# Second LayerNorm of rows 512 to 1023: from the tail into the segment loop

## The chip, the core and the metric

The kernel runs on one core of one Trainium2 chip. The metric is the device time of one execution in microseconds (us); smaller is better. The engines named below are PE (TensorE, matmuls; PEld is its weight load), DVE (VectorE), ACT (ScalarE), POOL (GpSimd) and SP (SyncE, which here only issues DMAs).

## The reference

What is computed is one transformer layer on x, 2048 rows of 640, in bf16. The first half is attention with a recurrent memory: the rows are taken in 64 segments of 32, each segment's 8 memory rows are the first 8 output rows of the segment before, so the segments must run one after the other. The second half is a LayerNorm and a gated feed-forward network over all rows.

```python
for s in range(n_seg):                      # 64 segments of 32 rows, in order
    h = concat([mem, layernorm(x)[segment s]])
    q, k, v = h @ Wq, h @ Wk, h @ Wv        # 32 heads of 128
    o = softmax(mask(q @ k.T * scale)) @ v @ Wo
    mem = o[:, :8]                          # goes into segment s + 1
    outs.append(o[:, 8:])
h  = x + concat(outs)                       # 2048 x 640
n  = layernorm(h)                           # the second LayerNorm
h2 = h + (relu(n @ W_gate) * (n @ W_up)) @ W_down     # 640 -> 1728 -> 640
```

## The kernel before

Every operation is recorded with the tiles that it reads and writes (`add`, `dma`), and `_Graph.solve` turns these into semaphore waits. Each engine then runs its own operations strictly in the order in which they were recorded. So the order of the Python statements is the order of each queue, SP's among them: a DMA that has to wait holds up every DMA recorded behind it on SP.

**The segment loop** (L1119 to L1297) runs s from 1 to 63, straight-line code, one segment a step. A step projects the keys (L1157), finishes the previous segment's attention over its own rows (`pv_x`, L1172, which reads V through the tile VM), projects the queries and values, takes scores, and multiplies with Wo (`wo_split`, `wo_pass`). The chain from one step to the next goes through `fold_split` (L635): DVE transposes into TA (L637), ACT copies into SA (L639), POOL or DVE adds (L641), and `to_act_split` (L650) writes the 8 memory rows of the next step's input. VM is filled by DMAs from SP (`merge_v`, L683, called at L1235): three DMAs, due at `pv_x` of the next step. PE is kept filled within a step by other work (`filler`, and matmuls that `fill_of` splits in two).

**Early row groups.** Rows 0 to 511, as four groups of 128 rows, get their second LayerNorm inside this loop. A group begins at a step e of `EARLY` (L981) and takes five steps:

- step e, near its end (L1271): SP loads the group's x rows into xt and its attention output into at;
- step e + 1 (L1174): POOL adds them into xt (`add_attn`, L730), SP stores the sum to the DRAM tensor h_d, and at the end of the step DVE takes the row statistics (`row_moments`, L1285);
- step e + 2 (L1169): ACT and POOL scale the rows (`row_std`, `row_scale`);
- step e + 4 (L1242, L1269): SP transposes xt into at by a transposing DMA, and then stores at to the DRAM tensor xn2_d. The store writes runs of 128 elements.

The tile at is shared: the first LayerNorm's rows go through it in steps with s % 4 == 1, and the attention load of a group overwrites it.

POOL's other work in a step is `late_q` (L518, for the next step's scores), `late_o` (L598) and, where s % 4 is not 1, the addition L641 of the chain. In the order of POOL these stand behind `add_attn`, and on SP `merge_v` of the same step stands behind the store to h_d.

**The last steps.** From step 49 on xn2_d is read back (`early_rows`, L908) for early pieces of the first gate and up products, and before the end of the loop all of it goes into the tile xn2T0 (L1190).

**The tail.** The feed-forward part runs over four blocks of 512 rows. For block b, `gate_up(b, j)` makes 14 column tiles from the tile xn2T (L1014, L1027), and `down_pair` multiplies with Wd (L1311, L1324), adds the residual rows in h_rows (`down_out`, L1333) and stores. Block 1 takes its input from xn2T1 and its residual from h1. Its four row groups, 4 to 7, are prepared while block 0 runs: `ln2_load` brings x and the attention output (tiles xt2, at2), `ln2_front` adds, takes statistics and scales (DVE L730, L356, L358, L370, ACT L361, L363), `ln2_back` transposes into xn2T1 by a transposing DMA (L375). The calls for groups 4 to 7 stand at L1403, L1415, L1416, L1431, L1440, L1441, L1450 and L1451, between the gate and up products of block 0, its weight loads (`load_down`, `load_piece`) and its down products. Blocks 2 and 3 are prepared in the same manner during blocks 1 and 2 (L1423, L1442); the change leaves these alone.

Of the kernel before, what the change touches and what calls it, by code (L numbers as in the profile page):

```python
# [5 lines left out]
BF16 = mybir.dt.bfloat16  # L6
# [171 lines left out]
def build_kernel(nc, A_x, A_mem0, A_Wq, A_Wk, A_Wv, A_Wo, A_seg_len, B_W_gate, B_W_up, B_W_down, out):  # L178
    _, S, D = A_x.shape
# [6 lines left out]
    DC = D // 128  # L186
# [8 lines left out]
    CH = [8 * g + 4 * hf + f for hf in range(2) for g in range(4) for f in range(4)]  # L195

    x_ap, out_ap, mem0_ap = A_x[0], out[0], A_mem0[0]
    h_d = nc.dram_tensor("h_d", [TB, D], BF16)
    xn2_d = nc.dram_tensor("xn2_d", [128, DC, TB], BF16)
    attn_d = nc.dram_tensor("attn_d", [S, 4, DC * 32], BF16)  # L200
    ends_d = nc.dram_tensor("ends_d", [128, 64 * H + 8 * VW], BF16)
    NE = 7
# [148 lines left out]
    def dma(dst, src, r=(), w=(), eng="sp"):  # L351
        add(eng, lambda e: e.dma_start(dst, src), r=r, w=w, dma=True)  # L352
# [384 lines left out]
    def ln2_load(i):  # L737
        u = i % 4
        dma(xt2[u][:, :], x_ap[128 * i:128 * i + 128, :], r=[("Wdone", 1)], w=[("xt2", u)])
        load_attn(at2[u], i, [("Wdone", 1)], ("at2", u))  # L740

    def ln2_front(i):
        par, u = (i // 4) % 2, i % 4
        h, hk = h_rows[par][:, u, :], ("h", par, u)
        add_attn(h, xt2[u], at2[u], [("xt2", u), ("at2", u)], [hk])
        row_stats(h, hk, 128)
        row_scale(h, hk, 128, xt2[u], ("xt2", u))
# [160 lines left out]
    def early_rows(q, lo, hi):  # L908
        ks = [XHOME[q][c][1] for c in range(lo, hi)] + ([("Ve1", q)] if hi == DC else [])
        if q:  # L910
            dst = ends[:, 512 * lo:512 * hi].rearrange("p (c t) -> p c t", t=512)
        elif hi == DC:
            dst = XHOME[0][4][0].rearrange("p (c t) -> p c t", t=512)
        else:
            dst = (Ke[0], Qe[0])[lo // 2][:].rearrange("p h t -> p (h t)").rearrange("p (c t) -> p c t", t=512)
        dma(dst, xn2_d[:, lo:hi, :], r=[("xn2_d", u) for u in range(4)], w=ks)

    def early_tile(s, q):
        return ((xt, ("xt",)), (at, ("at",)) if s < NSEG - 7 else (xl, ("xl",)))[q]
# [58 lines left out]
                    flip(2 + i, (Qe, Ke)[j][p], i, [(("Qe", "Ke")[j], p, i)])  # L978
        return part, evac

    EARLY = (15, 23, 31, 39)  # L981

    def woe_sum(bk):

# [134 lines left out]
    for s in range(1, NSEG):  # L1119
# [16 lines left out]
        if s > 0:  # L1136
            a, ks = pass_act(s)
            held, parts = fill_of(s)
            if s in (NSEG - 14, NSEG - 13, NSEG - 10, NSEG - 9, NSEG - 5, NSEG - 4):
                early_weights(s, 1)  # L1140
            elif s in (NSEG - 12, NSEG - 8):
                q = 1 - place(s)[0]
                for n in range(2):
                    dma((ends[:, 1024 * n:1024 * n + 1024] if q else (Ke, Qe)[n][0][:].rearrange("p h t -> p (h t)")),
                        next_d[2 * q + n][:, :], r=[("next", 2 * q + n)] + [("next", 3, i) for i in range(2) if q * n],
                        w=[(("Ke", "Qe")[n], q, i) for i in range(2)])
                add("pool", lambda p, q=q: p.memset(ap(Ve[q], Dh, [[VW, 8], [1, VW - Dh]]), 1.0),
                    w=[("Ve1", q), ("Ve", q, 0), ("Ve", q, 1)])
            elif s == NSEG - 3:
                for n in range(2):  # L1150
                    dma(ends[:, 1024 * n:1024 * n + 1024], ends_d[:, 1024 * n:1024 * n + 1024], r=[("ends",)],
                        w=END_KEYS[2 * n:2 * n + 2])
            elif s == 1:
                dma(ends_d[:, :], ends[:, :], r=END_KEYS, w=[("ends",)])
                far_save(0)
                far_save(1)
            for i in range(2):  # L1157
                project(a, ks, 1, (i,), ((P2, P3)[i],), *WAYS[i], held=i == 1 and held[0], parts=parts[i])
                to_tok((P2, P3)[i], i, "act")
                if last and i == 1:  # L1160
                    load_piece(("Ko", 0), "act")
                flip(i, Ko, i, [("Ko", i)])
            if s == 1:
                row_std(n_rows(1))
                row_scale(xl, ("xl",), n_rows(1), xl, ("xl",), "pool")
            if s % 4 == 2 and more:
                row_std(n_rows(nb + 1))
                row_scale(xl, ("xl",), n_rows(nb + 1), xl, ("xl",), "pool")
            if s % 4 == 1 and e2 is not None:  # L1169
                row_std(128)  # L1170
                row_scale(xt, ("xt",), 128, xt, ("xt",), "pool")
            pv_x(s - 1, 0)  # L1172
            norm_x(0)
            if s % 4 == 0 and e2 is not None:  # L1174
                add_attn(xt[:, :], xt, at, [("xt",), ("at",), ("rx",)], [("xt",)], "pool")
                dma(h_d[128 * e2:128 * e2 + 128, :], xt[:, :], r=[("xt",)], w=[("h_d", e2)])
            if s % 4 == 2:
                merge_v(s, 1)
            if not last:
                for i in range(2):  # L1180
                    project(a, ks, 0, (i,), ((P0, P1)[i],), *WAYS[i], held=i == 1 and held[1], parts=parts[2 + i])
                    to_tok((P0, P1)[i], 2 + i, "act")
                    flip(2 + i, Qo, i, [("Qo", i)])
                    if i == 0:
                        norm_x_late(0)
                        flip_ox(s - 1, (0,))
            else:
                norm_x_late(0)
                flip_ox(s - 1, (0,))
            if s == NSEG - 2:  # L1190
                for n, (lo, hi) in enumerate(((0, 1), (1, 2), (2, 3), (3, DC))):
                    dma(xn2T[0][:, lo:hi, :], xn2_d[:, lo:hi, :], r=[("xn2_d", u) for u in range(4)] + [("Wdone", 0)],
                        w=[("xn2", 0, n)])
            project(a, ks, 2, (0,), (P2,), range(4), held=not last and held[2])
            scores(s, 0, (0, 1))
            project(a, ks, 2, (0,), (P2,), (4,))
            scores(s, 0, (2, 3))
            if not last:
                exp_mem(s, 0)
                first_exp = G.ops[-1]  # L1200
                mask_mem(s, 0)
            to_v(P2, Vp, 0, ("Vp",), "act")
            if last:
                load_piece(("Vp", 0), "act")
            if s % 4 == 1 and ln:
                flip_rows(chunks_of(at[:, :]), xl, ("xl",), ("at",))
                if more:
                    ln1_load(nb + 1, xl, ("xl",))
                    G.ops[-1].after = first_exp
            if s in (NSEG - 15, NSEG - 11, NSEG - 7):  # L1210
                early_weights(s + 1, 0)
                G.ops[-1].after = first_exp
                early_rows(1 - place(s + 1)[0], 2, 4)
            elif s == NSEG - 3:
                dma(ends[:, 2048:], ends_d[:, 2048:], r=[("ends",)], w=END_KEYS[4:])
# [151 lines left out]
    def load_down(n):  # L1367
# [3 lines left out]
        if n == 4:  # L1371
            for q in range(2):
                dma(Wd[FR * q:FR * q + FR, FC - 1, :], B_W_down[FM:F, :], r=r, w=[("Wd", 5 + q)])

    s = NSEG - 1

    def rows(bk, p, s):
# [22 lines left out]
    flip_ox(s)  # L1400
    late_o(s)
    gate_up(0, NE + 2)
    ln2_load(4)  # L1403
    dma(hT[0][:, 0:NE, :], hx_d[:, :, :], r=[("Wdone", 2)] + [("hx", n) for n in range(NE)],
        w=[("hT", 0, n) for n in range(NE)])
    load_down(2)
# [5 lines left out]
            r=[("Wt", q, 0)], w=[("Wt", q, 1)])  # L1412
    load_down(3)
    load_down(4)
    ln2_load(5)  # L1415
    ln2_front(4)  # L1416
    rows(P2, (s + 1) % 2, s)
    woe_pass(P3, range(16))
    woe_sum(P3)
# [2 lines left out]
    for b in range(NBLK):  # L1422
        if 0 < b < NBLK - 1:  # L1423
            for u in range(4):
                ln2_load(4 * (b + 1) + u)
        for j in range(FC):
            p = j - NE if b == 0 else j
            if b or p > 3:
                gate_up(b, j)
            if b == 0 and p in (4, 5):  # L1430
                ln2_load(p + 2)  # L1431
            if b == 0 and p == 5:
                dma(h_rows[0][:, :, :], h_d[:, :].rearrange("(u p) d -> p u d", p=128), r=[("h_d", u) for u in range(4)] +
                    [("Wdone", 1), ("hT", 0, j)], w=[("h", 0, u) for u in range(4)])
            if b == 0 and p in (5, 6):
                load_piece(("hT", 0, j - 1))
                load_piece(("hT", 0, j - 1))
            if b == 0 and p in (4, 5):
                if p == 4:
                    ln2_front(5)  # L1440
                ln2_back(p, None)  # L1441
            if 0 < b < NBLK - 1:  # L1442
                fronts, backs = (1, 3, 5, 7), (3, 5, 7, 9)
                if p in fronts:
                    ln2_front(4 * (b + 1) + fronts.index(p))
                if p in backs:
                    ln2_back(4 * (b + 1) + backs.index(p), None)
        if b == 0:
            for u in (6, 7):
                ln2_front(u)  # L1450
                ln2_back(u, None)  # L1451
        assert not pieces
        for n in range(2):
            down_pair(b, n)
# [63 lines left out]
```

## Time and profile before

| what | value |
|---|---|
| three runs | 988.79, 989.08 and 992.45 us; median 989.08 us |
| profiled execution | span 990.5 us from first to last instruction; the page gives no other time for it |
| PE busy | 962.9 us, 97% |
| DVE, ACT, POOL busy | 714.3, 522.2 and 171.7 us |
| steps of the loop | about 12.1 us each |

The profile shows one execution. Its page gives the busy time of each engine, a strip of 40 slices of the span, the DMA queues, the chain of work that ended last, and groups of instructions by line; views of the trace behind it show the instructions in order of time, who waited for whom, and busy times in chosen stretches. The span lies 1.4 us above the median of the three runs and inside their range, so differences below are worked out inside this execution and then taken off the median.

### The profile page before, as it was taken

What the parts mean: (1) busy time and instruction counts of PE and PEld (TensorE: products, weight loads), DVE (VectorE), ACT (ScalarE), POOL (GpSimd) and SP (SyncE); (2) the same over time, 40 slices, a digit from 0 to 9 for tenths busy, and PEclk for the clock granted to TensorE, in tenths of its full rate; (3) what the DMA queues carried; (4) which work ended last, traced back from release to release, by engine and by line L of the source; (5) the groups of instructions that cost most, each with busy time, mean ns of one, the idle gap of its engine ahead of it and who ended that gap; (6) DMA issues with size and microseconds to landing.
All of it is one profiled execution on the core that took longest, in us unless ns stands there. A gap on an engine that the chain in (4) does not pass through costs nothing.

```text
span 990.5 us, 56552 instructions
## 1 busy us (share of the span) xinstructions
PE 962.9 (97%) x26159; PEld 530.9 (54%) x24953; DVE 714.3 (72%) x1860; ACT 522.2 (53%) x1326; POOL 171.7 (17%) x420
## 2 busy tenths in 40 slices
PE   4889999999999999999999999999999999999998
PEld 1335555555555656555555555555555565344443
DVE  3668787878887888788888878787877775545332
ACT  1456666666666666666666666656555552122120
POOL 7121112121302131213021302020201110000000
PEclk9999999999999999999999999999999999999999
DMA  9951112121222122212221221132323348613100
GB/s 358 416 200 39 43 40 48 34 54 49 54 42 54 50 59 45 54 49 54 42 54 49 54 47 49 35 106 61 103 62 99 84 129 255 203 21 94 27 14 27
DMA packets 84562, 83.10 MB, mean 84 GB/s; under 512 B 49562, under 2 KB 68834, under 8 KB 82402
## 3 DMA queue, kind: packets, MB, share of 16 engines
q1 hardware_dynamic: 82592, 78.53, 27.3%
q8 instruction: 201, 3.29, 1.3%
q10 hardware_dynamic: 1730, 0.96, 0.4%
q14 instruction: 39, 0.32, 0.1%
HBM read 44.02 MB, written 9.31 MB: 54 GB/s over the span
## 4 chain that ended last, share of the span: by engine, by line
PE 89%; SPq 5%; DMA 3%; DVE 2%; issue 1%; ACT 0%; POOL 0%; DVEq 0%; ACTq 0%; POOLq 0%
PE ps L414 46%; PE ps L1014 9%; PE ps L609 7%; PE ps L626 7%; PE ps L387 6%; SPq L352 5%; PE ps L669 3%; PE ps L1311 2%; PE ps L510 2%; PE ps L698 2%; DMA Wo<-in_A_Wo_dram 2%; PE ps L904 2%; PE ps L563 2%; DMA xn2T<-xt 1%; DMA VM<-Vp 0%
## 5 line engine op out<-in xcount | busy, mean ns | idle before, releaser
L414 PE MATMUL ps<-W,act_r 128*32 128x512 bf16 (+1 forms) x8383 | 462.2, 358 | 1.2 <-DVE act_r L650 0.8
L414 PEld LDWEIGHTS ps<-W,act_r 128*32 128x32 bf16 x8383 | 214.7, 96 | 171.3 <-DVE act_r L650 30.6
L438 ACT ACTIVATE tok<-ps 128x512 bf16<-128x512 f32 x182 | 105.2, 594 | 57.5 <-PE ps L414 50.6
L433 DVE STREAM_TRANSPOSE Ko<-tox 128x512 bf16<-128x512 bf16 x128 | 89.9, 703 | 44.3 <-ACT tox L438 44.0
L438 ACT ACTIVATE tox<-ps 128x512 bf16<-128x512 f32 x138 | 81.8, 598 | 62.3 <-PE ps L414 49.4
L414 PE MATMUL ps<-W,act_e 128*32 128x512 bf16 x1056 | 103.3, 383 | 4.1 <-DVE TBf L491 1.9
L589 DVE STREAM_TRANSPOSE oT<-tox 128x512 bf16<-128x512 bf16 x128 | 95.4, 745 | 0.0
L433 DVE STREAM_TRANSPOSE Qo<-tok 128x512 bf16<-128x512 bf16 x124 | 85.5, 689 | 1.2 <-ACT tok L438 0.5
L609 PE MATMUL ps<-Wo,oT 128*32 128x160 bf16 x4032 | 81.4, 233 | 3.1 <-DMA Wo<-in_A_Wo_dram 3.1
L626 PE MATMUL ps<-Wo,oT 128*32 128x320 bf16 x2016 | 79.8, 299 | 0.3 <-issue 0.3
L609 PEld LDWEIGHTS ps<-Wo,oT 128*32 128x32 bf16 x4032 | 70.4, 97 | 13.2 <-DMA Wo<-in_A_Wo_dram 3.7
L438 ACT ACTIVATE Vp<-ps 128x512 bf16<-128x512 f32 x127 | 75.2, 592 | 0.5 <-ACT Vp L438 0.5
L387 PE MATMUL ps<-W,act_e 128*32 128x512 bf16 x744 | 73.3, 384 | 0.0
L639 ACT ACTIVATE SA<-TA 64x40 f32<-64x40 f32 x126 | 29.5, 234 | 75.3 <-DVE TA L637 74.6
L1042 ACT ACTIVATE g<-ps 128x512 bf16<-128x512 f32 x45 | 26.1, 593 | 73.8 <-PE ps L1014 72.3
L526 ACT ACTIVATE Pm<-ps 128x64 bf16<-128x64 f32 x126 | 28.1, 223 | 67.0 <-PE ps L510 66.9
L583 DVE STREAM_TRANSPOSE oT<-om 128x128 bf16<-128x128 bf16 x126 | 39.2, 311 | 31.0 <-ACT om L575 31.0
L626 PEld LDWEIGHTS ps<-Wo,oT 128*32 128x32 bf16 x2016 | 53.2, 96 | 15.5 <-DVE rm L573 0.8
L510 PE MATMUL ps<-Qo,Ko 128*32 128x40 bf16 x2048 | 61.1, 181 | 0.0
L510 PEld LDWEIGHTS ps<-Qo,Ko 128*32 128x32 bf16 x2048 | 46.2, 94 | 25.8 <-DVE Qo L433 18.3
L1043 DVE TENSOR_TENSOR hT<-g,ps 128x512 bf16<-128x512 bf16 x45 | 30.9, 687 | 39.7 <-PE ps L1014 35.7
L518 POOL COPY Qo<-ends 128x256 bf16<-128x256 bf16 x32 | 14.0, 439 | 259.6 <-DVE oT L583 242.1
(159 smaller groups left out, 1494.6 us busy)
## 6 DMA issues: line engine op xcount, KB each, us to landing
VM<-Vp SPq DMA_DIRECT2D x126, 65.0 KB
VM<-Vp SPq DMA_DIRECT2D x63, 130.0 KB
W<-in_A_Wk_dram SPq DMA_DIRECT2D x5, 1024.0 KB
W<-in_A_Wq_dram SPq DMA_DIRECT2D x5, 1024.0 KB
W<-in_A_Wv_dram SPq DMA_DIRECT2D x5, 1024.0 KB
Wo<-in_A_Wo_dram SPq DMA_DIRECT2D x8, 640.0 KB
attn_d<-wtok SPq DMA_DIRECT2D x248, 7.5 KB
xt<-in_A_x_dram SPq DMA_DIRECT2D x16, 160.0 KB
```

The source lines that it names most:

```text
L352: add(eng, lambda e: e.dma_start(dst, src), r=r, w=w, dma=True)
L387: return pe.add_instruction(mybir.InstMatmult(name=nc.get_next_instruction_name(), engine=mybir.EngineType.PE, ins=[pe.lower_ap(rhs), pe.l ...
L414: ins = pe.matmul(*b, start=(c == ends[0]), stop=(c == ends[1]), skip_group_check=True)
L433: add("dve", lambda v: v.transpose(dst[:, 16 * i:16 * i + 16, 0:32], tok[t][:, :].rearrange("p (h f) -> p h f", f=32)), r=tok_keys(t), w=keys)
L438: add("act", lambda a: a.activation(dst, src, ACTF.Copy), r=r, w=w)
L510: i = pe.matmul(bank((P0, P1)[hf])[q:q + 32, o:o + 40], (Ko if a == 0 else Ke[p])[:, h, :], Qo[:, h, :], start=True, stop=True, skip_group ...
L583: add("dve", lambda v: v.transpose(ap(oT[par], 160 * hf, [[40, 4], [320, 4], [1, 8]]), ap(om, 128 * hf, [[1, 4], [4, 32]])), r=[("om", hf) ...
L589: add("dve", lambda v, kh=kh: v.transpose(ap(oT[p], 160 * kh + M, [[320, 4], [40, 4], [1, 32]]), ap(tox, 128 * kh, [[256, 4], [1, 4], [4, ...
L609: i = pe.matmul(bank(bk)[32 * gg:32 * gg + 32, 0:160], src[:, hb, 0:32], w[:, gg], start=(hb == CH[16 * halves[0]]), stop=(hb == CH[-1]), ...
L626: i = pe.matmul(bank(bk)[32 * q:32 * q + 32, 0:320], src[:, hb, 0:32], w, start=(n == 0), stop=(n == 7), skip_group_check=True)
L1014: ins = pe.matmul(bank(bk), w[:, c, lo:lo + 128], xn2T[par][:, c, :], start=(c == 0), stop=(c == DC - 1))
L1043: add("dve", lambda v: v.tensor_tensor(hT[par][:, j, :], g1[gi][:, :], bank(bu), ALU.mult), r=[B(bu), ("g1", gi)], w=[("hT", par, j)])
```

## The change

Four more groups, rows 512 to 1023, are prepared in the loop: `EARLY` gets a group every four steps from 15 to 43, where it had one every eight from 15 to 39. h_d and xn2_d grow to 1024 rows; reads of the first block's part of xn2_d take the slice 0:TB. In the tail, everything that prepared groups 4 to 7 goes (the loads, the additions, statistics and scaling, the transposes), and two DMAs take its place: one loads xn2T1 whole from xn2_d, one loads h1 from h_d. With the new spacing a group's last step is the first step of the next one: the transpose and the store of the one and the loads of the other then stand one behind the other on SP.

```diff
-    h_d = nc.dram_tensor("h_d", [TB, D], BF16)
-    xn2_d = nc.dram_tensor("xn2_d", [128, DC, TB], BF16)
+    h_d = nc.dram_tensor("h_d", [2 * TB, D], BF16)
+    xn2_d = nc.dram_tensor("xn2_d", [128, DC, 2 * TB], BF16)
...
-        dma(dst, xn2_d[:, lo:hi, :], r=[("xn2_d", u) for u in range(4)], w=ks)
+        dma(dst, xn2_d[:, lo:hi, 0:TB], r=[("xn2_d", u) for u in range(4)], w=ks)
...
-    EARLY = (15, 23, 31, 39)
+    EARLY = tuple(range(15, 47, 4))
...
-                    dma(xn2T[0][:, lo:hi, :], xn2_d[:, lo:hi, :], r=[("xn2_d", u) for u in range(4)] + [("Wdone", 0)],
+                    dma(xn2T[0][:, lo:hi, :], xn2_d[:, lo:hi, 0:TB], r=[("xn2_d", u) for u in range(4)] + [("Wdone", 0)],
...
+    def load_rows(b, r):
+        dma(h_rows[b][:, :, :], h_d[TB * b:TB * b + TB, :].rearrange("(u p) d -> p u d", p=128),
+            r=[("h_d", 4 * b + u) for u in range(4)] + r, w=[("h", b, u) for u in range(4)])
...
     gate_up(0, NE + 2)
-    ln2_load(4)
     dma(hT[0][:, 0:NE, :], hx_d[:, :, :], r=[("Wdone", 2)] + [("hx", n) for n in range(NE)],
...
     load_down(4)
-    ln2_load(5)
-    ln2_front(4)
+    dma(xn2T[1][:, :, :], xn2_d[:, :, TB:2 * TB], r=[("Wdone", 2)] + [("xn2_d", u) for u in range(4, 8)],
+        w=[("xn2", 1, u) for u in range(4)])
     rows(P2, (s + 1) % 2, s)
...
-            if b == 0 and p in (4, 5):
-                ln2_load(p + 2)
             if b == 0 and p == 5:
-                dma(h_rows[0][:, :, :], h_d[:, :].rearrange("(u p) d -> p u d", p=128), r=[("h_d", u) for u in range(4)] +
-                    [("Wdone", 1), ("hT", 0, j)], w=[("h", 0, u) for u in range(4)])
+                load_rows(0, [("Wdone", 1), ("hT", 0, j)])
...
-            if b == 0 and p in (4, 5):
-                if p == 4:
-                    ln2_front(5)
-                ln2_back(p, None)
...
         if b == 0:
-            for u in (6, 7):
-                ln2_front(u)
-                ln2_back(u, None)
+            load_rows(1, [("Wdone", 2), ("hT", 0, FC - 1)])
```

## The prediction

> **What bounds the kernel now.** I read the page first, then the time lost by PE in each stage, then the waits at the places where it is lost. The page's first lines are the span and the busy times:
>
> ```profile
> span 990.5 us, 56552 instructions
> PE 962.9 (97%) x26159; PEld 530.9 (54%) x24953; DVE 714.3 (72%) x1860; ACT 522.2 (53%) x1326; POOL 171.7 (17%) x420
> ```
>
> PE leaves 27.6 us of the span. The view by stages (start and end, length, then the busy time of PE, PEld, DVE, ACT and POOL, then the granted clock, the DMA share and GB/s) says where:
>
> ```profile
> 0.00:51.20 51.20, 34.35 (x625) 11.23 (x416) 24.86 (x62) 17.24 (x35) 21.12 (x102) 1.00 0.98 388
> ...
> 51.20:636.60 585.40, 580.59 (x18605) 339.29 (x17910) 474.84 (x1274) 363.24 (x937) 122.15 (x249) 1.00 0.21 53
> ...
> 830.00:880.00 50.00, 47.18 (x258) 19.85 (x205) 27.53 (x60) 11.79 (x31) 0.91 (x2) 0.97 0.54 157
> ```
>
> Most idle time (16.85 us) is in the first stage, loading weights, which the change doesn't touch. In the loop PE is busy for 580.59 of 585.40 us. Between 830 and 880 us it loses 2.82 us, and there alone the clock is below 1.00. The removed work sits there. The waits of 830 to 856 us (engine, line, what it waited for; us in total, times, longest) name the two idle places:
>
> ```profile
> PE ps L1014 <- DMA xn2T<-xt: 2.4, 1, 2.4
> ...
> PE ps L1311 <- DVE hT L1043: 0.4, 1, 0.4
> ```
>
> The first is the opening gate product of block 1, which waits for the last transposed group of xn2T1. PE in order of time there, and the stages around it:
>
> ```profile
> 852.50 2.29 PE L1014 MATMUL ps<-xn2T,Wg 128*128 128x512 bf16 x5 [2.44 <-DMA xn2T<-xt]
> 854.58 1.93 PE L1014 MATMUL ps<-xn2T,Wu 128*128 128x512 bf16 x5
> 856.34 1.24 PE L1014 MATMUL ps<-xn2T,Wg 128*128 128x512 bf16 x5
> 857.42 1.24 PE L1014 MATMUL ps<-xn2T,Wu 128*128 128x512 bf16 x5
> ```
>
> ```profile
> 850.10:852.50 2.40, 0.00 (x0) 0.03 (x1) 0.89 (x2) 0.00 (x0) 0.00 (x0) 1.00 0.71 233
> 852.50:856.00 3.50, 3.50 (x9) 1.31 (x10) 0.89 (x2) 0.60 (x1) 0.00 (x0) 0.51 0.36 110
> ```
>
> So the wait costs twice. It is 2.44 us of idle time, and right behind it the granted clock is 0.51 for 3.5 us. A group of five matmuls starts 857.42 - 856.34 = 1.08 us after the one before at full clock; the two slow groups take 854.58 - 852.50 = 2.08 and 856.34 - 854.58 = 1.76, together 1.68 us too much.
>
> **The change part by part.**
>
> *The tail.* Removed are four chains of load, addition, statistics, scaling and transpose. Their instructions on DVE, in order of time:
>
> ```profile
> 834.61 0.49 DVE L730 TENSOR_TENSOR h<-xt,at 128x640 bf16<-128x640 bf16 x1 [2.62 <-DMA at<-attn_d]
> ...
> 836.94 0.45 DVE L370 TENSOR_SCALAR xt<-h,mv,rs 128x640 bf16<-128x640 bf16 x1 [0.67 <-ACT rs L363]
> 837.42 0.69 DVE L1043 TENSOR_TENSOR hT<-g,ps 128x512 bf16<-128x512 bf16 x1
> ```
>
> and on SP (start, time to issue):
>
> ```profile
> 832.14 0.57 SPq L352 DMA_DIRECT2D at<-attn_d  x1
> ...
> 838.98 1.04 SPq L352 DMA_DIRECT2D Wg<-in_B_W_gate_dram  x2
> 840.07 1.54 SPq L375 DMA_TRANSPOSE xn2T<-xt  x1
> 841.65 1.22 SPq L352 DMA_DIRECT2D Wu<-in_B_W_up_dram  x2
> 842.91 4.33 SPq L375 DMA_TRANSPOSE xn2T<-xt  x2
> ```
>
> Group 5's chain stands ahead of the product L1043 on DVE, which ran only at 837.42; that made PE's idle 0.38 us (the 0.4 above). With the chain gone this wait goes: **-0.38 us**. The last transposes, issued from 842.91 behind the weight pieces, made the 2.44 us. They are replaced by one load of xn2T1, recorded behind `load_down`, before the statements that run at 832 us. Its data (four groups of 160 KB, 640 KB) were stored in the loop, so nothing holds it. What is late next for PE at 850.06? The weight pieces of group 3, 672 + 448 + 672 + 448 KB = 2240 KB. In all 640 (xn2T1) + 640 (h0) + 2240 + 640 (h1) = 4160 KB have to move from 831 us on. At 270 GB/s, what the core moved with transposes among its DMAs, that is 15.8 us, to 847:
>
> ```profile
> 834.30:850.10 15.80, 15.38 (x114) 5.25 (x60) 9.04 (x22) 2.73 (x9) 0.00 (x0) 1.00 0.90 270
> ```
>
> h1 comes last and isn't wanted before block 1's down product, so the pieces are there at about 845, some 5 us early. The wait goes: **-2.44 us**, and with it the half clock: **-1.68 us**. Sum of the tail: -4.50 us. No other idle time of PE near it can go, so this is also about the most that can be won.
>
> [...]
>
> *The loop, as the groups stand now.* The old kernel has groups at steps 15, 23, 31 and 39, and steps between them that have almost none of this work. The transposes into TA (L637) of steps 15, 19, 23 and 27:
>
> ```profile
> 238.45 0.52 DVE L637 STREAM_TRANSPOSE TA<-ps 128x320 f32<-128x320 f32 x1
> ...
> 286.79 0.52 DVE L637 STREAM_TRANSPOSE TA<-ps 128x320 f32<-128x320 f32 x1
> ...
> 335.07 0.52 DVE L637 STREAM_TRANSPOSE TA<-ps 128x320 f32<-128x320 f32 x1
> ...
> 383.26 0.52 DVE L637 STREAM_TRANSPOSE TA<-ps 128x320 f32<-128x320 f32 x1
> ```
>
> Four steps with a group's work take 48.34 and 48.19 us, the four without 48.28 us. So DVE's statistics, ACT's two small activations, POOL's addition and scaling and the added DMAs are hidden beside PE's matmuls: **0 us** for four more, within 0.1 us a group.
>
> *The loop, where two groups now meet.* This the old trace does not show. At steps 19, 23, ... 43 (seven times) a transpose and a store are followed on SP by the next group's loads. The store must have landed before the attention load may overwrite at. SP around step 19, and the old addition and POOL's queue:
>
> ```profile
> 286.78 1.28 SPq L375 DMA_TRANSPOSE at<-xt  x1
> 290.79 0.63 SPq L352 DMA_DIRECT2D xn_d<-at  x1
> 291.46 2.99 SPq L352 DMA_DIRECT2D attn_d<-wtok  x4
> 296.99 1.83 SPq L352 DMA_DIRECT2D VM<-Vp  x3
> ```
>
> ```profile
> 244.16 1.41 POOL L730 TENSOR_TENSOR xt<-xt,at 128x640 bf16<-128x640 bf16 x1 [4.28 <-DVE rx L710]
> ...
> 298.66 0.43 POOL L518 COPY Qo<-Qe 128x256 bf16<-128x256 bf16 x1 [10.44 <-DVE oT L583]
> 299.15 0.40 POOL L598 COPY oTe<-oT 128x256 bf16<-128x256 bf16 x1
> 300.02 0.27 POOL L641 TENSOR_TENSOR SA<-SA,TA 128x40 f32<-128x40 f32 x1 [0.47 <-ACT SA L639]
> ```
>
> The store is issued at 290.79. The DMA strip of 290.7 to 294.7 us, in slices of 0.1 us, has its bulk from 291.9 to 292.9 and stragglers until 294.7:
>
> ```profile
> GB/s 0 0 0 0 0 0 0 0 0 0 164 0 0 15 172 210 207 207 202 207 195 162 28 0 0 8 8 8 10 8 10 13 18 18 67 19 0 0 51 26
> ```
>
> So the attention load is issued at 294.7 at the latest. In the tail such a load took 834.61 - 832.14 = 2.5 us until DVE could use it: 297.2. The addition takes 1.41: 298.6, just when POOL's copy L518 is due (298.66). The store to h_d, 0.35 us on SP, stands behind the addition, and the three VM loads behind that: they start at 299.0 instead of 296.99, **2.0 us late**. Their last bytes moved at 300.0 in the strip of 296.9 to 300.9 us (slices of 0.1 us):
>
> ```profile
> GB/s 0 0 0 0 0 0 0 0 0 0 0 0 0 229 291 104 42 0 0 166 374 458 271 63 0 104 187 270 83 21 164 0 0 0 0 0 0 0 0 0
> ```
>
> that is 302.0 now, and 302.2 with 0.2 us to land. PE wants VM at 302.92:
>
> ```profile
> 302.92 0.29 PE L698 MATMUL ps<-VM,Px 64*32 64x129 bf16 x11
> ```
>
> A cover of 0.7 us is left of 2.7, and on POOL the 0.47 us before L641. By the normal row the cost is 0, the lower end. The upper end is a slow landing. At step 53 the same loads were issued from 695.99 to 697.82 and PE had to wait until 701.35:
>
> ```profile
> 695.99 1.83 SPq L352 DMA_DIRECT2D VM<-Vp  x3
> ...
> 701.35 0.23 PE L698 MATMUL ps<-VM,Px 64*32 64x129 bf16 x3 [0.26 <-DMA VM<-Vp]
> ```
>
> 3.5 us behind the end of the issue, against 300.0 + 0.2 - 298.82 = 1.4: 2.1 us slower, 1.4 us over the cover, and 1.4 x 7 = 10 us if all seven do so. The traffic that slows it is irregular, and the normal row is nearer; I take 0.3 us in three of the seven steps: **+1.0 us**, ends 0 and +10.
>
> *Reads of xn2_d.* Its runs are cut from two chunks to one (1 KB). That touches the loads of steps 49, 53 and 57, which stand ahead of the VM loads; only step 53 has no cover, as just seen. One more descriptor a partition: **+0.2 us**, ends 0 and +0.5.
>
> Sum: -0.38 - 2.44 - 1.68 + 0 + 1.0 + 0.2 = **-3.3 us**. The profiled span would go from 990.5 to 987.2, the median from 989.08 to **985.8 us**.
>
> **The rivals.**
>
> *SP and POOL as the new bound* (slower). The meeting of two groups holds POOL's addition, the h_d store and VM back past 302.92 in every such step. For it: the cover is 0.7 us and the DMA latencies spread by 2 us. Against it: the rows around step 19 still fit. It takes more than (4.5 - 0.2) / 7 = 0.61 us in each of the seven steps to lose the whole gain; at the upper end of 10 us the result is 989.08 - 4.5 + 10 + 0.2 = 994.8. Typical 991.
>
> *The half clock stays.* If it isn't brought on by this gap, the gain is 1.68 us smaller: 987.5 us. For it: no other gap of this length is in the tail to compare; against it: it begins with the first matmul after the gap.
>
> *The wait only changes its name.* xn2T1 or the weight pieces land after 850 us. Then the tail gains 0.38 us and the loop's 1.2 us is lost: 989.9. Against it the 5 us of room.
>
> *The median run has less of it to lose.* The profiled execution is 1.4 us over the median. If the usual execution waits shorter, the gain is smaller by up to 1.4: about 987.2.
>
> **How the numbers follow.** Chances: the forecast (the meeting of groups costs 0 to 2.5 us: 984.8 to 987.3, with half a microsecond of spread on either side) 0.57; SP and POOL 0.20, a third of it over 994.0; half clock stays 0.09; wait renamed 0.05; less to lose 0.09. A measurement of this kernel can tell 0.5% (4.9 us) from no change. Faster by more needs 984.1 or less: the whole tail and 0.4 us beyond it, 0.09. Slower by more, over 994.0: 0.07. Within: 0.84. The range reaches from 984.0 (all of the tail, no loss, and the spread) to 990.5, which leaves out the worse half of the first rival.
>
> **What would show it.** Right: no idle time of PE before L1014 of block 1, starts 1.08 us apart from its first group on, clock 1.00 from 830 to 880 us; steps 20, 24, ... 44 as long as the others within 0.3 us. Wrong: idle time before L698 named VM, or POOL's L641 later than ACT's L639, in those seven steps; or L1014 waiting for Wg or xn2T.

## The result, and the profile after

| what | before | after |
|---|---|---|
| median of 6 runs each | 988.97 us (988.04 to 992.45) | 992.88 us (992.22 to 994.57) |
| ratio | | 1.0039, 95% interval 1.0026 to 1.0052 |
| span of the profiled execution | 990.5 us | 990.9 us (its own time 992.66 us) |

The change costs 3.9 us, 0.39%. I had forecast a gain of 3.3 us and a range of 984.0 to 990.5 us.

The two spans differ by 0.4 us only, the medians by 3.9. The profiled execution after took 992.66 us with a span of 990.9, so 1.8 us lie around a span; the profiled execution before, with 990.5, was then one of about 992.3 us, 3.3 us above its median. A span must not be set against a median without these 1.8 us, and comparisons with this one profile give the kernel before too much to lose.

The first lines of the page after:

```profile
span 990.9 us, 56548 instructions
PE 960.6 (97%) x26146; PEld 530.2 (54%) x24953; DVE 715.9 (72%) x1852; ACT 522.9 (53%) x1326; POOL 187.8 (19%) x428
```

POOL has 16 us more, as it should with four more groups, and DVE has not less but 1.6 us more, though it has eight instructions fewer. The stages tell why. First the kernel before, cut at L637 of steps 12, 48 and 62 (columns as in the prediction):

```profile
202.20:636.60 434.40, 434.40 (x13998) 255.27 (x13468) 356.09 (x958) 270.79 (x701) 93.98 (x189) 1.00 0.21 50
636.60:805.80 169.20, 168.94 (x5403) 100.01 (x5296) 132.99 (x358) 100.58 (x260) 24.49 (x62) 1.00 0.33 86
805.80:990.60 184.80, 179.04 (x1550) 80.41 (x1339) 81.59 (x168) 41.13 (x95) 3.90 (x9) 0.99 0.32 96
```

and the same stages of the kernel after:

```profile
201.40:641.70 440.30, 435.15 (x13994) 254.88 (x13464) 365.98 (x969) 273.00 (x709) 109.93 (x197) 1.00 0.26 57
641.70:810.30 168.60, 168.60 (x5402) 99.89 (x5294) 132.72 (x358) 100.79 (x260) 24.54 (x62) 1.00 0.34 86
810.30:991.00 180.70, 176.25 (x1540) 80.08 (x1343) 73.56 (x148) 39.32 (x87) 3.98 (x9) 1.00 0.31 94
```

The tail is 4.1 us shorter, the steps 13 to 48 are 5.9 us longer, and there PE, which had no idle time at all, now has 5.15 us of it. DVE's busy time in these steps grew by 9.9 us, where the twelve added instructions of four groups make 4.2 (360.27 - 356.09 in the last version below, which has the same instructions and none of the long steps).

Who the idle time in the loop belongs to is seen in the view of the line L532, DVE's mask product (`mask_mem`; Pm and mbd, its two operands, both lie in SBUF). In the kernel after:

```profile
L532 DVE TENSOR_TENSOR Pbd<-Pm,mbd x252: 180/215/1419, 43.7 to 808.5; 128x128 bf16<-128x128 bf16 x126
...
  PE ps L563: 5.9, 7
```

180/215/1419 are its shortest, median and longest duration in ns, and the lower row says that PE waited for it 5.9 us in 7 places. The kernel before has, in the same view:

```profile
L532 DVE TENSOR_TENSOR Pbd<-Pm,mbd x252: 180/216/241, 43.9 to 803.9; 128x128 bf16<-128x128 bf16 x126
...
  PE ps L563: 0.9, 1
```

So an instruction of 0.2 us takes up to 1.42 us. Six of the seven waits, 5.0 us, lie in steps 13 to 48, in steps 20, 24, 28, 32, 36 and 40, where the kernel before has none: they are nearly all of the 5.15 us that PE is idle there. Step 20 of the kernel after, DVE and then POOL, in order of time:

```profile
285.86 0.52 DVE L637 STREAM_TRANSPOSE TA<-ps 128x320 f32<-128x320 f32 x1
...
294.49 0.32 DVE L532 TENSOR_TENSOR Pbd<-Pm,mbd 128x128 bf16<-128x128 bf16 x2
...
295.87 1.50 DVE L532 TENSOR_TENSOR Pbd<-Pm,mbd 128x128 bf16<-128x128 bf16 x2
...
299.08 0.52 DVE L637 STREAM_TRANSPOSE TA<-ps 128x320 f32<-128x320 f32 x1
```

```profile
295.76 1.40 POOL L730 TENSOR_TENSOR xt<-xt,at 128x640 bf16<-128x640 bf16 x1 [8.46 <-DMA at<-attn_d]
```

POOL's addition, which had to wait for the attention load, starts 0.11 us before the second pair of mask products and ends at 297.16; the pair, 0.32 us at 294.49, takes 1.50 and ends 0.21 us after the addition. The step lasts 299.08 - 285.86 = 13.22 us instead of 12.07.

### The profile page after: what moved, and what is told of

It reads as the page before. It is cut to its first block, busy times and chain, and to the rows that moved or that the text cites. A ratio compares the mean times of both kernels' runs of the same rounds, so it can differ in the third digit from the quotient of the medians.

```text
span 990.9 us, 56548 instructions
## 1 busy us (share of the span) xinstructions
PE 960.6 (97%) x26146; PEld 530.2 (54%) x24953; DVE 715.9 (72%) x1852; ACT 522.9 (53%) x1326; POOL 187.8 (19%) x428
## 4 chain that ended last, share of the span: by engine, by line
PE 88%; DVE 5%; SPq 3%; DMA 2%; ACT 1%; issue 1%; POOL 0%; DVEq 0%; ACTq 0%; POOLq 0%
PE ps L414 43%; PE ps L1014 9%; PE ps L609 7%; PE ps L387 7%; PE ps L626 7%; PE ps L669 4%; SPq L352 3%; PE ps L1311 3%; PE ps L904 2%; PE ps L510 2%; DMA Wo<-in_A_Wo_dram 2%; PE ps L698 2%; PE ps L563 2%; DVE Pbd L532 1%; DVE oT L589 1%; DVE Qo L433 1%
## 5 line engine op out<-in xcount | busy, mean ns | idle before, releaser
L433 DVE STREAM_TRANSPOSE Ko<-tox 128x512 bf16<-128x512 bf16 x128 | 89.9, 703 | 39.8 <-ACT tox L438 39.5
L433 DVE STREAM_TRANSPOSE Qo<-tok 128x512 bf16<-128x512 bf16 x124 | 85.4, 689 | 0.8
L609 PE MATMUL ps<-Wo,oT 128*32 128x160 bf16 x4032 | 81.5, 233 | 2.2 <-DMA Wo<-in_A_Wo_dram 2.1
L609 PEld LDWEIGHTS ps<-Wo,oT 128*32 128x32 bf16 x4032 | 70.4, 97 | 12.4 <-DMA Wo<-in_A_Wo_dram 3.2
L1311 PE MATMUL ps<-Wd,hT 128*128 128x320 bf16 (+4 forms) x225 | 57.9, 299 | 0.0
```

Of the source, the lines that this page charges most:

```text
L433: add("dve", lambda v: v.transpose(dst[:, 16 * i:16 * i + 16, 0:32], tok[t][:, :].rearrange("p (h f) -> p h f", f=32)), r=tok_keys(t), w=keys)
L609: i = pe.matmul(bank(bk)[32 * gg:32 * gg + 32, 0:160], src[:, hb, 0:32], w[:, gg], start=(hb == CH[16 * halves[0]]), stop=(hb == CH[-1]), ...
L1311: i = pe.matmul(*a, start=(j == 0), stop=(j == FC - 1), skip_group_check=True)
```

## The experiments

My theory after this view: POOL's addition and DVE's product of two SBUF operands shut each other out, and the late attention load pushed the one onto the other (**theory 1**). The rivals are that the traffic of the DMAs costs the time, or VM and the rest of SP's queue as I had forecast (**theory 2**); and for the tail, that the usual execution has less to lose there than the profiled one.

**The tail alone, and the loop alone.** Tail alone keeps four groups in the loop and loads block 1's tiles from the first half:

```diff
-    EARLY = tuple(range(15, 47, 4))
+    EARLY = (15, 23, 31, 39)
-    dma(xn2T[1][:, :, :], xn2_d[:, :, TB:2 * TB], r=[("Wdone", 2)] + [("xn2_d", u) for u in range(4, 8)],
+    dma(xn2T[1][:, :, :], xn2_d[:, :, 0:TB], r=[("Wdone", 2)] + [("xn2_d", u) for u in range(4)],
...
-        dma(h_rows[b][:, :, :], h_d[TB * b:TB * b + TB, :].rearrange("(u p) d -> p u d", p=128),
+        dma(h_rows[b][:, :, :], h_d[0:TB, :].rearrange("(u p) d -> p u d", p=128),
...
```

> The tail of the change alone: four groups in the loop as before, and block 1 takes its two tiles by DMA from the rows of the first half (rows 512 to 1023 of the output are therefore made from the wrong input rows; sizes, instructions and transfers are those of the change). If the tail brings what I predicted: 4.5 us less than before, 984.5 us, no wait before the first gate product of block 1 and clock 1.00. If the median execution before has less to lose there: 0.5 to 3 us less, 986 to 988.5. If loads in the tail collide anew: not faster than 988.5.

Measured: 986.91 us, ratio to the kernel before 0.9967 (0.9953 to 0.9982). The tail brings 2.2 us, as the second expectation had it. Loop alone takes `EARLY` and the larger DRAM tensors of the change into the kernel before:

> The loop of the change alone: eight groups in the loop, and the tail prepares groups 4 to 7 itself as before (done twice, the result of the loop is not used). The profile after shows six steps longer by 0.5 to 1.2 us, 5.9 us in all, each with PE waiting at the memory product (L563) for a mask product of DVE (L532) of up to 1.42 us instead of 0.2. If that is the loss of the change: 5.5 to 6.5 us more than before, 994.5 to 995.5 us, the same six steps. If part of the loss needs the new tail: less than 4 us more.

Measured: 994.71 us, ratio 1.0056 (1.0041 to 1.0071), 5.6 us more. -2.2 and +5.6 make +3.4, the change has +3.9; the difference is within the intervals. The loss lies in the loop and doesn't need the new tail. The long steps are not the same six: here steps 20, 36 and 44 have the long mask product (L532 up to 1.40 us), and in others the addition comes still later and takes another way to the chain. The waits behind the addition of step 24, between 346 and 351 us:

```profile
DVE act_r L650 <- POOL SA L641: 1.5, 1, 1.5
PE ps L414 <- DVE act_r L650: 1.3, 1, 1.3
```

There the addition began 0.10 us behind L637, POOL's copies L518 and L598 and the sum L641 had to queue behind it, and PE waited for the next step's memory rows. Once, behind the addition of step 28, PE waited 0.2 us for VM. What decides is when the addition starts, counted from L637 of the step before, over the profiles of the change and of the loop alone:

| start of the addition, us after L637 | steps | step longer by | longest L532 |
|---|---|---|---|
| 5.71 (as before) | 16 | 0.0 us | 0.22 us |
| 9.24, 9.43, 9.58, 9.67 | 40, 20, 24, 32 | 0.51, 0.70, 0.85, 0.95 | 0.72, 0.91, 1.06, 1.15 |
| 9.82 to 10.07 | 44, 20, 36, 36, 28 | 1.10 to 1.21 | 1.29 to 1.42 |
| 10.27 to 10.40 | 44, 40, 28 | 0.0, in loop alone 0.33 and 0.40 in the step after | 0.22 |
| 11.71, 12.2 | 32, 24 | 1.26 and 1.64, in the step after | 0.22, 0.24 |

The later the addition begins, the longer the product is held, until the product has gone first.

**No addition.**

```diff
-                add_attn(xt[:, :], xt, at, [("xt",), ("at",), ("rx",)], [("xt",)], "pool")
-                dma(h_d[128 * e2:128 * e2 + 128, :], xt[:, :], r=[("xt",)], w=[("h_d", e2)])
+                if s == 16:
+                    add_attn(xt[:, :], xt, at, [("xt",), ("at",), ("rx",)], [("xt",)], "pool")
+                dma(h_d[128 * e2:128 * e2 + 128, :], xt[:, :], r=[("xt",), ("at",), ("rx",)], w=[("h_d", e2)])
```

> The change, but in the seven steps where two groups meet POOL does not add the attention output into xt (the second half of the layer then lacks the attention there); all loads, stores and their waits stay, the store to h_d still waits for the attention load. Theory 1, that POOL's late addition and DVE's mask product shut each other out: L532 stays under 0.25 us, steps 20 to 44 are all 12.0 to 12.2 us, 5.9 us less than the change, 987.0 us. Theory 2, that the DMA traffic that now falls into that part of the step, or the late VM loads, hold DVE or PE: at least 4 of the 5.9 us stay, 991 us or more.

Measured: 989.18 us, ratio to the kernel before 1.0000 (0.9985 to 1.0016), 3.7 us less than the change, with all its DMAs and waits in place. Only the seven additions are left out. The mask product never exceeds 0.23 us:

```profile
L532 DVE TENSOR_TENSOR Pbd<-Pm,mbd x252: 177/215/226, 44.6 to 803.5; 128x128 bf16<-128x128 bf16 x126
```

The median lies between the two expectations, 2.2 us above theory 1's 987.0 us and 1.8 us below theory 2's 991: without the additions 3.7 us of the loss go, and 2.3 us over the tail alone stay. So the mask product is held by the addition, as theory 1 says, but the addition isn't shown to be the whole price. In the profiled execution (987.67 us, the fastest of ten) no step from 13 to 48 is long, so what the slower ones lose isn't seen there.

**VM first.** Twice, the store to h_d is recorded behind `merge_v(s, 0)`: in the change, and in the kernel without the addition.

> The change with the store of the sum to h_d put behind the three VM loads on SP instead of ahead of them. My forecast's route (the late addition holds up VM): the VM loads are issued 10.2 us after L637 again, and 3 us or more of the 3.9 us loss go. Theory 1 (addition against mask product): the same steps stay long by 0.5 to 1.2 us, L532 up to 1.4 us, less than 1.5 us less than the change, 991.5 to 993 us.

Measured: 993.25 us, ratio 1.0048 (1.0029 to 1.0067): nothing gained over the change, though the VM loads were early again (issued from 345.59, with PE reaching for them at 352.70). L532 still takes up to 1.43 us. The route of my forecast is not where the change loses its time.

> Both: no addition by POOL in the seven steps (the second half of the layer lacks the attention there) and the store to h_d behind the VM loads. Without the addition alone the median was 989.18 us, 2.3 us above the tail alone, though the profiled execution, at 987.67, showed no long step. If late VM loads in other executions make these 2.3 us: 986.9 us. If they come from elsewhere: 988.5 us or more.

Measured: 988.62 us, ratio 0.9993 (0.9981 to 1.0004), 1.7 us above the tail alone: as the second expectation had it, the time comes from elsewhere. Late VM loads may make 0.6 of the 2.3 us, which the intervals don't settle; the rest stays open. In the profiled execution (988.79 us) one step of the loop, 34, is 0.8 us longer; PE is idle there for 0.66 us before L609, and the profile shows nothing that it waited for.

**Doses.** In the kernel before, without any added DMA, an extra POOL instruction starts just ahead of the second pair of mask products in twelve steps:

```diff
+    DOSES = {20: ("add", 640), 21: ("add", 320), 22: ("add", 160), 28: ("copy", 640), 29: ("copy", 320), 30: ("add", 640),
+             36: ("fill", 640), 37: ("fill", 320), 38: ("copy", 640), 44: ("add", 480), 45: ("fill", 640), 46: ("add", 320)}
...
         exp_mem(s, 1)
+        dose(s)
```

> The kernel before with twelve extra POOL instructions of different length and kind on the idle tile xt, each started when the exponentials of the second half (Pm) are done, that is just ahead of DVE's second mask product L532; no DMA is added. Steps 20, 21, 22, 30, 44, 46: a sum of two SBUF operands over 640, 320, 160, 640, 480, 320 columns; steps 28, 29, 38: a copy of 640, 320, 640 columns; steps 36, 37, 45: a fill, which reads nothing, of 640, 320, 640. Theory 1, that a POOL instruction shuts DVE's two-operand product out until it ends: with the sums L532 grows with the number of columns, to about 1.1 to 1.4 us at 640, half of that at 320, and the step with it. [...] Theory 2, DMA traffic: L532 stays at 0.2 us in all twelve.

One execution was measured, the profiled one, 991.61 us. POOL at steps 20, 21, 28 and 45, then DVE's pairs at the same places:

```profile
295.87 1.25 POOL L1126 TENSOR_TENSOR xt<-xt 128x640 bf16<-128x640 bf16 x1 [8.31 <-ACT Pm L526]
```
```profile
308.75 0.72 POOL L1126 TENSOR_TENSOR xt<-xt 128x320 bf16<-128x320 bf16 x1 [8.28 <-ACT Pm L526]
```
```profile
393.60 0.72 POOL L1128 COPY xt<-xt 128x640 bf16<-128x640 bf16 x1 [8.29 <-ACT Pm L526]
```
```profile
600.81 0.63 POOL L1130 MEMSET xt<- 128x640 bf16 x1 [8.28 <-ACT Pm L526]
```
```profile
296.13 1.21 DVE L532 TENSOR_TENSOR Pbd<-Pm,mbd 128x128 bf16<-128x128 bf16 x2
```
```profile
309.01 0.67 DVE L532 TENSOR_TENSOR Pbd<-Pm,mbd 128x128 bf16<-128x128 bf16 x2
```
```profile
393.88 0.65 DVE L532 TENSOR_TENSOR Pbd<-Pm,mbd 128x128 bf16<-128x128 bf16 x2
```
```profile
601.09 0.35 DVE L532 TENSOR_TENSOR Pbd<-Pm,mbd 128x128 bf16<-128x128 bf16 x2
```

The sum of 640 columns runs until 297.12, and the pair ends at 297.34; of 320 columns until 309.47, and the pair ends at 309.68; the copy until 394.32, the pair 394.53. In each the pair ends 0.21 to 0.22 us after POOL, which is the time of its second product: the first one waits for the end of the POOL instruction, whatever its length. All nine sums and copies show it, from a first product of 0.25 us beside 0.45 us on POOL to 1.08 us beside 1.25 us, and none of the three fills does (0.21 us). The fill of step 45 runs until 601.44 and the pair beside it takes its usual 0.35 us. The four steps are longer by 0.87, 0.31, 0.32 and 0.02 us than their usual length. So it is neither POOL being busy as such, since the fill of 0.63 us held nothing, nor the DMAs, since none was added: what held the product were the nine instructions that read xt in SBUF (0.45 to 1.25 us), and not the three that only write it. Why reading makes the difference is not shown. Whether a product that has begun also holds a POOL instruction is not shown here.

**The store one step earlier.** The edit is made in the change:

```diff
-        e2c = EARLY.index(s - 4) if s - 4 in EARLY else None
+        e2c = EARLY.index(s - 3) if s - 3 in EARLY else None
```

> The change with a group's transpose and store to xn2_d one step earlier, at step e + 3, so that the tile at is free when the next group's loads are issued at step e + 4. Theory 1: POOL's addition starts 5.7 us after L637 of the step before in all eight groups, as in the kernel before, L532 stays at 0.22 us, steps 20 to 44 are 12.0 to 12.2 us, and what is left is the gain of the tail: as the tail alone, 986.9 us. Theory 2, that the amount of DMA traffic in the loop is what costs: 989 us or more.

Measured: 987.60 us, ratio 0.9988 (0.9975 to 1.0000). Step 20's addition:

```profile
291.04 1.41 POOL L730 TENSOR_TENSOR xt<-xt,at 128x640 bf16<-128x640 bf16 x1 [4.27 <-DVE rx L710]
```

It waits for DVE's rx again and not for the load, 5.7 us after L637, as in all eight groups, and L532 never exceeds 0.23 us. Its stages, steps 13 to 48 and the tail:

```profile
200.80:635.40 434.60, 434.43 (x14002) 254.91 (x13472) 360.27 (x969) 272.97 (x709) 110.10 (x197) 1.00 0.27 57
804.10:985.20 181.10, 177.35 (x1550) 79.92 (x1340) 73.44 (x148) 39.32 (x87) 3.94 (x9) 1.00 0.32 95
```

All eight groups, with the whole DMA traffic of the change, cost the loop 0.2 us in this profiled execution (986.95 us, one of the fastest of eleven). By the medians this version is 5.3 us faster than the change, and 1.4 us under the kernel before, with an interval that ends at no difference; 0.7 us above the tail alone. So the traffic as such is not what costs. It gains 1.6 us more than leaving the additions out did; where those come from is not shown.

**The kernel before again, three times**, to size the tail.

> The kernel before, unchanged, for a second profile of it. The first profile has a span of 990.5 us; the profile after has a span of 990.9 us in an execution of 992.66 us, so about 1.8 us lie around a span, and the first profile would belong to an execution of 992.3 us, 3.3 us above the median of 988.97. Theory that the median execution has less to lose in the tail: the second profile has a span near 987 us, and the 2.44 us wait of the first gate product of block 1, or the 3.4 us of half clock behind it, are shorter or not there. Rival, that the difference lies at the start (weight loading) or in single steps of the loop: span near 987 us, and both are there as before, to 0.3 us.

> The kernel before, unchanged, a third profile. The tail alone brought 2.2 us where I had 4.5. Two profiles of the kernel before differ: in the first PE waited 2.44 us before the first gate product of block 1 and then had half clock (1.68 us), in the second it waited 1.95 us and kept the clock, and 0.66 us before the down product instead of 0.38. If the half clock is the exception: no half clock behind the wait, wait and the down product's wait together 2 to 3 us, span near 987 us. If it is the rule: half clock in this profile and in the fourth.

> The kernel before, unchanged, a fourth profile, to count with the third: as stated there, exception (no half clock, the waits of the tail 2 to 3 us together) or rule (half clock again, 4 us or more together).

Times 989.08, 989.04 and 989.76 us, spans 987.3, 987.3 and 988.0 us. PE's waits at the transition, one fence for each of the three:

```profile
PE ps L1014 <- DMA xn2T<-xt: 1.9, 1, 1.9
...
PE ps L1311 <- DVE hT L1043: 0.7, 1, 0.7
```
```profile
PE ps L1014 <- DMA xn2T<-xt: 1.7, 1, 1.7
...
PE ps L1311 <- DVE hT L1043: 0.4, 1, 0.4
```
```profile
PE ps L1014 <- DMA xn2T<-xt: 1.1, 1, 1.1
...
PE ps L1311 <- DVE hT L1043: 0.4, 1, 0.4
```

2.6, 2.1 and 1.5 us together, the last below the 2 to 3 us expected, and in none the clock falls behind the wait (1.00 in each); in the second profile the stage behind it reads:

```profile
851.20:855.00 3.80, 3.79 (x18) 1.76 (x18) 1.58 (x3) 1.17 (x2) 0.00 (x0) 1.00 0.44 144
```

The mean, 2.1 us, is near what the tail alone brought (2.2). The first profile, on which I worked, had 2.8 us of waiting, the most of the four, and alone had half clock behind it (1.68 us). Such executions seem to recur. Its mean clock is 0.998; of the 48 further runs of the kernel before, measured beside the experiments, seven have 0.998 or less, and six of these took 991.07 us or more, against medians of 989.08 and 989.03 us.

## Why the prediction was wrong

**What bounds the tail: right in kind.** The two waits of PE that I named are gone after the change, as I had said, and the opening products of block 1 follow each other at 1.08 us with no wait for a DMA:

```profile
854.24 1.03 PE L1014 MATMUL ps<-xn2T,Wg 128*128 128x512 bf16 x4 [0.16 <-issue]
855.10 1.24 PE L1014 MATMUL ps<-xn2T,Wu 128*128 128x512 bf16 x5
856.18 1.03 PE L1014 MATMUL ps<-xn2T,Wg 128*128 128x512 bf16 x4
```

The weight pieces were there, as worked out. The rival "The wait only changes its name" did not come about.

**-0.38, -2.44 and -1.68: mis-sized.** I had 4.50 us from the first profiled execution; the medians give 2.2. I saw that the span stood 1.4 us above the median and gave the rival "less to lose" 1.4 us; with the 1.8 us around a span the execution stood 3.3 us above it. The half clock, the largest part of the difference, was neither bound to stay nor, in most executions, a thing to win: the clock is 1.00 from 830 to 880 us in the profile after, and three more profiles of the kernel before don't have the half clock.

**0 for the groups as they stand: right.** Where they don't meet at the shared tile, steps 13 to 48 take 434.6 us with eight groups against 434.4 with four.

**+1.0 where two groups meet: the step that failed.** "The addition takes 1.41: 298.6, just when POOL's copy L518 is due." The chain up to there was about right: counted from L637 the attention load was issued 7.6 us after it (forecast 7.9) and the addition started at 9.9 (forecast 10.4). But I then looked only at what stands behind the addition on POOL and behind its store on SP, and not at what runs beside it on DVE. The row that I took the addition from has it 5.7 us after L637, beside DVE instructions that read PSUM or one operand (L711, L433 and L716, at their usual 0.69, 0.71 and 0.39 us); shifted by 4 us it takes the same 1.40 us, but lies on the mask product and holds it. The term of +1.0 was to pay for late landings of VM, and nothing in it for DVE. Measured in its place: 0.5 to 1.2 us in six of the seven steps, 5.9 us in the profile after, 5.6 us in the loop alone, against 1.0. Of this 3.7 us go by the medians when the additions are left out; how the rest divides is open.

**+0.2 for the reads of xn2_d: not seen.** Steps 49 to 62 took 168.6 us after and 169.2 us before; no run here shows a price for the shorter runs of xn2_d. The 0.2 us were an estimate of mine with no row behind it.

**SP and POOL as the new bound**, the rival on the slower side, had the right steps, the right instruction (POOL's late addition) and a price (a typical 991 us) that fell 1.9 us short, but not the way: VM was in time in all seven steps of the profile after, and putting it first gained nothing. Its ways do exist, as loop alone showed where a load landed later still: through L641 in two steps, and through VM for 0.2 us in one. It had a chance of 0.20; the range up to 990.5 cut it off in the middle.

## What to carry to other kernels

When an instruction moves in time, look up what runs beside it at its new place on the other engines, not only what queues behind it on its own: here POOL's addition of 1.40 us, which reads SBUF, held DVE's product of two SBUF operands until it ended, for up to 1.42 us instead of 0.2. When a stage is reused at a shorter period, its last step meets the next one's first: move the store that frees the shared tile ahead of the load that needs it (5.3 us less here). And before the gain is sized from one profile, set its span plus what lies around a span against the median: here half of a gain of 4.5 us belonged to one long execution.

## What the runs showed that I had not expected

- A POOL sum or copy of bf16 operands that started just ahead held DVE's mask product of two SBUF operands (0.2 us) until it ended: 1.07 to 1.43 us with POOL instructions of 1.25 to 1.40 us, 0.52 to 0.54 us with ones of 0.72 us. A fill of 0.63 us didn't hold it (0.21 us). DVE's transposes (L433, 0.71 us) and its products with one operand in PSUM (L711, 0.69 us) ran beside the four 1.41 us additions of the kernel before at their usual durations (0.66 to 0.71 and 0.69 us in all steps).
- In four profiles of the kernel before the half clock came once, behind a wait of 2.44 us, and not behind waits of 1.9, 1.7 and 1.1 us at the same place. In the first profile the clock is 0.50 for 3.41 us, from 852.55 to 855.96 us, and 1.00 in the stretches on either side, 849.13 to 852.55 us, which holds the wait, and 855.96 to 860.00 us. What made it fall there, the length of the wait or something else, four profiles with one such case don't show.
